# A planner that orders five engines is told other durations for its transfers

## The chip, the cores and the metric

The program runs on one core of one Trainium2 chip. The metric is the device time of one execution in microseconds (us). The matrix engine is called PE here, VectorE DVE, ScalarE ACT, GpSimd POOL, and SyncE, which issues all the transfers, SP.

## What is computed

```python
def _attn_ref(q, k, v):                      # (8, 12, 448, 64) float32 each
    scores = np.matmul(q, k.transpose(0, 1, 3, 2)) / np.sqrt(64) - np.log(448)
    return np.matmul(1.0 / (1.0 + np.exp(-scores)), v)
...
x = attn.transpose(0, 2, 1, 3).reshape(8, 448, 768)
h = x.transpose(0, 2, 1) @ U @ V             # U (448, 32), V (32, 448)
u = x + h.transpose(0, 2, 1)
y = u + np.maximum(u @ w_ch1, 0.0) @ w_ch2   # (768, 3072) and (3072, 768)
```

Sigmoid attention over 8 batches of 12 heads, a mixing of rank 32 along the sequence, and a feed-forward with a residual.

## The kernel before

**Stages.** The two feed-forward weights come as 48 pieces of 128x768 words (w_in), are decoded on DVE and ACT, split in two float16 halves and written to memory (scratch). Attention goes batch by batch in six pairs of heads. A pair of batches 0 to 2 is multiplied in float32; a pair of batches 3 to 7 (30 pairs) is first staged: four loads of keys and queries into a `qk` buffer (three of them) and loads of the values; on ACT a bound of each (L469, into `junk`); the bounds go out to memory (`far`, 128x3 words) and come back as one row on all partitions (`row`, 128x384, a single buffer); DVE reduces that row (L448), and after three small operations POOL and DVE write a high and a low float16 half of queries, keys and values into one of two `stg` buffers. PE then makes the scores, ACT the sigmoid (`at`, L675) and the high halves of the weights (`a`, L698 and L701), DVE the low halves (L416 out of L700 and L703), PE the values, ACT copies them to `u` (L707).

The feed-forward of batches 0 to 3 runs in groups of the weights, 18 matmuls for each block in (`ffn_in`, evacuated by ACT at L934 and L935 and by DVE at L936) and 12 for each block out (`ffn_out`, added to `ua` or `ub` by DVE at L955, which shows as L416). Batches 4 and 5, then 6 and 7, go through products of seven by a Strassen scheme (`product`), whose weight forms are made by `quarter_sums` and whose inputs lie in `ufar` (L1063) and are loaded into the freed `qk` and other buffers (L1089) when the last scores are done.

**What sets the order.** Nothing is written by hand in its final order. `Plan.op` notes each operation with its engine, a told cost, what it reads and writes, and a position; `Plan.order` then steps through a simulated time: the engine that can start first takes, of its operations that are ready, the one with the lowest position. A transfer takes its cost on SP, then its `dma` time on one common pipe (L208), and is there `LAND` later. The result is a fixed order on each of the five engines and a fixed choice of buffers. On the chip every engine works through its own list, waiting at semaphores.

```python
op("SP", 0.6 if n in (...) else 0.36, ..., land=land, dma=max(0.2, n / RATE))    # load(), L387
load(lambda: far.x, lambda: parts.x[:, :n], 0.08e6, kp, [far], pos)               # scale_by_dma, L445
load(lambda: row.x[...], lambda: far.x..., 0.2e6, [far], [row], pos)              # L446
```

With `RATE` 0.33e6 bytes per us and `LAND` 2.2 us. The positions come from some 45 numbers at the head of the file (L54 to L73).

## Time and profile before

| | |
|---|---|
| median of 3 runs | 1577.08 us (1575.58 to 1581.07) |
| the profiled execution | 1587.46 us |
| its span, first to last instruction | 1585.7 us |
| mean granted clock of PE | 0.996 |
| busy: PE, DVE, ACT, POOL | 98%, 70%, 49%, 23% |
| moved by DMA | 303.82 MB, 192 GB/s on average |

The page lists busy time by engine and by line. A busy PE is no proof that it is not held up elsewhere, so the rows below go from windows of the span to the waits of PE, and from these to the timeline, in which the bracket behind an instruction gives the idle time of its engine before it and what ended it. Lines such as L403, L413 and L416 are helpers; tiles tell what an instruction belongs to.

### The profile page before, as it was taken

How to read it: one execution, taken by the hardware profiler on the slowest of the kernel's cores; microseconds unless marked ns; L12 is line 12 of the kernel's file. 1: busy time of each engine (PE TensorE's matmuls, PEld its weight loads, DVE VectorE, ACT ScalarE, POOL GpSimd, SP SyncE). 2: the span in 40 equal slices, each digit the busy share in tenths (PEclk: the TensorE clock that was granted, in tenths of full speed). 3: DMA queues.
4: the chain of work that ended last, by engine and by line, in shares of the span. 5: the costliest groups of instructions: out<-in, count | busy, mean ns of one | idle time of the engine just before them, and what ended most of it. 6: DMA issues, size and time to landing. Idle time of an engine off the chain costs nothing.

```text
span 1585.7 us, 23387 instructions
## 1 busy us (share of the span) xinstructions
PE 1556.3 (98%) x8651; PEld 761.4 (48%) x8651; DVE 1110.7 (70%) x1831; ACT 774.2 (49%) x1269; POOL 358.6 (23%) x429
## 2 busy tenths in 40 slices
PE   8999999999999999899899999999999999999999
PEld 2334444454444454444444445555555555555554
DVE  3688888476676577687678776687767677565656
ACT  5566456445665547677676772342333614131210
POOL 0110000014541453122213325045552500000000
PEclk9999999999999999999999999999999999999999
DMA  9599777345667875667578447968683664323321
GB/s 268 162 291 335 238 240 263 126 121 149 201 158 202 218 273 148 174 157 190 142 216 223 140 142 261 302 221 256 205 265 121 243 233 142 114 105 130 115 105 70
DMA packets 217554, 303.82 MB, mean 192 GB/s; under 512 B 138336, under 2 KB 188384, under 8 KB 206176
## 3 DMA queue, kind: packets, MB, share of 16 engines
q1 hardware_dynamic: 217440, 302.33, 62.7%
q8 instruction: 68, 1.11, 0.3%
q14 instruction: 46, 0.38, 0.1%
HBM read 232.10 MB, written 76.04 MB: 194 GB/s over the span
## 4 chain that ended last, share of the span: by engine, by line
PE 77%; DMA 11%; DVE 5%; SPq 3%; issue 2%; ACT 2%; POOL 0%; ACTq 0%; POOLq 0%; DVEq 0%
PE banks L403 76%; DMA far<-tiny 3%; DMA w<-w_in 2%; DMA row__114<-far 2%; SPq L387 2%; DMA forms<-scratch 1%; DVE a L416 1%; SPq L989 1%; DMA w<-parked 1%; ACT at L675 1%; DMA qk__101<-q_in 1%; DMA w__92<-scratch 1%; DVE stg__109 L416 1%; PE banks L406 1%; DMA forms<-xnt 0%
## 5 line engine op out<-in xcount | busy, mean ns | idle before, releaser
L403 PEld LDWEIGHTS <-w__92 128*128 128x128 f16 x1683 | 163.5, 98 | 158.1 <-issue 8.1
L403 PEld LDWEIGHTS <-w__91 128*128 128x128 f16 x1620 | 157.4, 98 | 152.1 <-issue 7.9
L403 PEld LDWEIGHTS <-w__94 128*128 128x128 f16 x1620 | 156.5, 98 | 153.8 <-issue 11.3
L403 PEld LDWEIGHTS <-w__93 128*128 128x128 f16 x1557 | 151.6, 99 | 155.5 <-issue 21.7
L675 ACT ACTIVATE at<-banks,tiny 128x896 f32<-128x896 f32 x120 | 128.1, 1097 | 46.3 <-DVE a L416 20.0
L403 PE MATMUL banks<-h__96,w__94 128*128 128x448 f16 x696 | 141.7, 353 | 0.7 <-ACT h__95 L935 0.5
L416 DVE SCALAR_TENSOR_TENSOR a<-at,a 64x896 f16<-64x896 f32 (+1 forms) x120 | 134.9, 1135 | 10.3 <-ACT a L701 4.8
L403 PE MATMUL banks<-h__95,w__93 128*128 128x448 f16 x657 | 136.7, 361 | 4.6 <-DVE ua__73 L416 4.5
L413 POOL TENSOR_SCALAR tiny<-tiny 128x1 f32<-128x1 f32 (+1 forms) x90 | 33.4, 381 | 388.9 <-DVE tiny L413 359.0
L1010 POOL TENSOR_TENSOR w<-w 128x384 f32<-128x384 f32 x96 | 105.5, 1099 | 5.4
L403 PE MATMUL banks<-us__90,w__91 128*128 128x448 f16 x501 | 101.9, 353 | 0.4 <-DVE ub__82 L416 0.4
L403 PE MATMUL banks<-us__90,w__92 128*128 128x448 f16 x498 | 101.5, 353 | 0.0
L403 PE MATMUL banks<-us__89,w__92 128*128 128x448 f16 x474 | 95.5, 353 | 1.5 <-ACT r__97 L934 1.5
L403 PE MATMUL banks<-us__89,w__91 128*128 128x448 f16 x474 | 96.0, 353 | 0.0
L701 ACT ACTIVATE a<-at 128x896 f16<-128x896 f32 x90 | 82.7, 947 | 0.2
L448 DVE TENSOR_REDUCE tiny<-row__114 128x3 f32<-128x384 f32 x30 | 20.2, 674 | 71.8 <-DMA row__114<-far 71.8
L675 ACT ACTIVATE a<-banks,tiny 128x448 f32<-128x448 f32 (+1 forms) x72 | 62.6, 910 | 12.6 <-PE banks L403 12.4
L1006 POOL TENSOR_TENSOR w<-w 128x384 f32<-128x384 f16 x48 | 46.2, 992 | 95.5 <-DVE xnt L1014 61.7
L1013 ACT CAST xnt<-w 128x1536 f16<-128x1536 f32 x24 | 35.2, 1469 | 40.5 <-POOL w L1010 23.3
L934 ACT ACTIVATE r__97<-banks 128x448 f32<-128x448 f32 x48 | 25.8, 538 | 57.7 <-PE banks L403 56.2
L403 PEld LDWEIGHTS <-stg__108 64*128 64x128 f16 (+1 forms) x690 | 32.8, 102 | 42.8 <-issue 21.2
L403 PE MATMUL banks<-h__95,w__94 128*128 128x448 f16 x258 | 52.4, 353 | 0.0
(896 smaller groups left out, 2864.2 us busy)
## 6 DMA issues: line engine op xcount, KB each, us to landing
w<-w_in SPq DMA_DIRECT2D x48, 768.0 KB, 6.9
forms<-xnt SPq DMA_DIRECT2D x24, 768.0 KB, 4.8
w__92<-forms SPq DMA_DIRECT2D x13, 1344.0 KB, 5.7
w__91<-forms SPq DMA_DIRECT2D x12, 1344.0 KB, 6.4
w__94<-forms SPq DMA_DIRECT2D x12, 1344.0 KB, 6.4
w__93<-forms SPq DMA_DIRECT2D x11, 1344.0 KB, 5.8
forms<-scratch SPq DMA_DIRECT2D x144, 96.0 KB, 4.9
w__91<-scratch SPq DMA_DIRECT2D x7, 1536.0 KB, 8.3
```

The source lines that it names most:

```text
L387: op("SP", 0.6 if n in (D * S * 4, D * D * 4, D * P * 4) else 0.36, lambda: nc.sync.dma_start(out=dst(), in_=src()), reads, writes, pos, l ...
L403: plan.made.append(nc.tensor.matmul(*x, **y))
L406: plan.made.append(nc.tensor.transpose(**x))
L413: return eng.tensor_scalar(out=out, in0=in_, scalar1=s1, scalar2=s2, op0=op0, **kw)
L416: return nc.vector.scalar_tensor_tensor(out=out, in0=in0, scalar=s, in1=in1, op0=op0, op1=op1)
L448: dve(0.15 + n * 0.175, lambda: nc.vector.tensor_reduce(out=m(), in_=row.x[:, : n * P].rearrange("q (p n) -> q n p", n=n), axis=AX.X, op=A ...
L675: act(cost, lambda: nc.scalar.activation(out_(), in_(), AF.Sigmoid, bias=bias_s, scale=c if whole else c.x), kin + ["bias"] + kc, kout, pos)
L701: act(0.95, lambda a=a, to=to: nc.scalar.activation(half(a, 0), to.x, AF.Copy, scale=A_UP), kto, [(a, 0)], here + A_OFF)
L934: act(0.54, lambda: nc.scalar.activation(r.x, ph.x[:, :S], AF.Relu, scale=DOWN_H), [ph], [r], pos - EV_IN)
L1006: pool(1.0, lambda j=j: nc.gpsimd.tensor_tensor(out=t.x[:, j], in0=quarter(j, 0), in1=quarter(j, 1), op=ALU.add), [(w, j, 0), (w, j, 1)] i ...
L1010: pool(1.0, lambda o_=o_, x=x, y=y, sub=sub: nc.gpsimd.tensor_tensor(out=t.x[:, o_], in0=t.x[:, x], in1=t.x[:, y], op=ALU.subtract if sub ...
L1013: act(1.45, lambda: nc.scalar.copy(o.x[:, :, :, 0], t.x.rearrange(order)), [(t, j) for j in range(4)], [(o, 0)], pos)
```

## The change

The operations, their dependencies and their number stay as they are. What the planner is told changes:

- `load` looks the pipe time up in a table `PIPE` by the byte count and falls back to the rate. The far and row loads are now given as P * 6 and P * 1536 bytes (768 and 196,608) and so find entries of 2.2 and 1.3 us instead of 0.24 and 0.61. A key or query load is 0.53 instead of 0.35, the small loads of 64x64 and 64x128 words 0.13 and 0.1 instead of 0.2, the values of a staged pair 1.3 (they have the row's byte count) instead of 0.60. The byte counts of a weight piece (P * PIECE * 8, 2.5 us) and of a store of weight forms (P * 24 * P * 2, 1.92 us) are the same number, 786,432, so that the second entry holds for both.
- Told costs of small operations on POOL and DVE are changed, most of them lowered.
- An engine may take an operation that is ready up to `HOLD` later than the first; this is 0.029 us on PE and 0 elsewhere.
- The numbers that set the positions are all new, and six of them (`B0` to `B5`) shift the begin of each later batch.

```diff
+PIPE = {P * PIECE * 8: 2.5, D * S * 4: 0.53, D * D * 4: 0.13, D * P * 4: 0.1, P * 2 * WE * 2: 4.8, P * 42 * P * 2: 4.1, P * 24 * P * 2: 1.92, P * 6: 2.2, P * 1536: 1.3}
-SWITCH, TURN, LAND, RATE = 0.09, -1.137, 2.2, 0.33e6
+SWITCH, TURN, LAND, RATE = 0.09, -2.054, 2.2, 0.33e6
+HOLD_PE, HOLD_DVE, HOLD_ACT, HOLD_POOL, HOLD_SP = 0.029, 0.0, 0.0, 0.0, 0.0
-PREP, BOUNDS, VALUES, SECOND, MIXED = 20.269, 8.551, 2.056, 3.976, 7.545
+PREP, BOUNDS, VALUES, SECOND, MIXED = 19.043, 11.533, 1.917, 3.17, 7.744
...
-            i = min((x[1], x[2]) for x in now if x[0] <= t + 1e-9)[1]
+            _, i, t = min((x[1], x[2], x[0]) for x in now if x[0] <= t + HOLD(e) + 1e-9)
...
-        op("SP", ..., land=land, dma=max(0.2, n / RATE))
+        op("SP", ..., land=land, dma=PIPE.get(n, n / RATE))
...
-        load(lambda: far.x, lambda: parts.x[:, :n], 0.08e6, kp, [far], pos)
-        load(lambda: row.x[:, : n * P], ..., 0.2e6, [far], [row], pos)
+        load(lambda: far.x, lambda: parts.x[:, :n], P * 6, kp, [far], pos)
+        load(lambda: row.x[:, : n * P], ..., P * 1536, [far], [row], pos)
...
-        pool(0.35, lambda: ts(nc.gpsimd, inv.x, x(), ...), [e], [inv], pos)
+        pool(0.28, lambda: ts(nc.gpsimd, inv.x, x(), ...), [e], [inv], pos)
...
-                pool(1.5, lambda t=t, cut=cut: scaled(w.x[:, 0, cut], t.x, s.x), [t, s], [hi], at)
+                pool(1.0, lambda t=t, cut=cut: scaled(w.x[:, 0, cut], t.x, s.x), [t, s], [hi], at)
...
-                begun_ = [MIDDLE - SOONER + NP * d * (i - BEND * i * ...) for i in (j, j + 1)]
+                begun_ = [MIDDLE - SOONER + NP * d * (i - BEND * i * ...) + (B0, B1, B2, B3, B4, B5)[i] for i in (j, j + 1)]
```

The order moves at many places: of PE's 856 blocks of matmuls 420 stand elsewhere, nearly all by a few places. Three places follow; in the rows `tiny` are columns of one small tile, `stg__108` and `stg__109` the two staging buffers, `banks` the accumulators. The lines of the changed kernel are 4 higher.

DVE at 651 to 663 us (before), where one pair's low halves are staged and the next pair's row is due; before:

```order
L416 SCALAR_TENSOR_TENSOR ua__73<-banks_110,tiny,ua__73 128x448
L448 TENSOR_REDUCE tiny<-row__114 128x3
L416 SCALAR_TENSOR_TENSOR ua__74<-banks_111,tiny,ua__74 128x448
L416 SCALAR_TENSOR_TENSOR stg__108<-qk__102,tiny,stg__108 128x512
L416 SCALAR_TENSOR_TENSOR stg__108<-qk__102,tiny,stg__108 128x448
L416 SCALAR_TENSOR_TENSOR a<-at,a 128x896 x2
L416 SCALAR_TENSOR_TENSOR stg__108<-v__105,tiny,stg__108 128x512
L413 TENSOR_SCALAR tiny<-tiny 128x3
```

now:

```order
L420 SCALAR_TENSOR_TENSOR ua__73<-banks_111,tiny,ua__73 128x448
L420 SCALAR_TENSOR_TENSOR stg__108<-qk__102,tiny,stg__108 128x512
L420 SCALAR_TENSOR_TENSOR stg__108<-qk__102,tiny,stg__108 128x448
L420 SCALAR_TENSOR_TENSOR a<-at,a 128x896 x2
L420 SCALAR_TENSOR_TENSOR stg__108<-v__105,tiny,stg__108 128x512
L438 TENSOR_REDUCE tiny<-banks_111 128x1
L940 TENSOR_TENSOR h__96<-r__97,h__96 128x448
L452 TENSOR_REDUCE tiny<-row__114 128x3
```

The reduction of the next pair's row went from ahead of the two key and query halves to behind them, two splits of weights, the values, a small reduction and an evacuation of the feed-forward.

DVE at 750 to 759 us, where `ua__73` is the evacuation of a feed-forward block out; before:

```order
L416 SCALAR_TENSOR_TENSOR stg__108<-qk__102,tiny,stg__108 128x512
L416 SCALAR_TENSOR_TENSOR stg__108<-qk__102,tiny,stg__108 128x448
L416 SCALAR_TENSOR_TENSOR stg__108<-v__105,tiny,stg__108 128x512
L448 TENSOR_REDUCE tiny<-row__114 128x3
L434 TENSOR_REDUCE tiny<-banks_111 128x1
L413 TENSOR_SCALAR tiny<-tiny 128x3
L416 SCALAR_TENSOR_TENSOR a<-at,a 128x896
L413 TENSOR_SCALAR tiny<-tiny 128x1
L416 SCALAR_TENSOR_TENSOR ua__73<-banks_111,tiny,ua__73 128x448
```

now, around the same reduction:

```order
L417 TENSOR_SCALAR tiny<-tiny 128x1
L940 TENSOR_TENSOR h__96<-r__98,h__96 128x448
L442 RECIPROCAL tiny<-tiny 128x1
L832 TENSOR_TENSOR tiny<-tiny 128x1
L420 SCALAR_TENSOR_TENSOR ua__75<-banks_110,tiny,ua__75 128x448
L420 SCALAR_TENSOR_TENSOR ua__76<-banks_111,tiny,ua__76 128x448
L420 SCALAR_TENSOR_TENSOR w_107<-uc__87,tiny,w_107 128x448
L420 SCALAR_TENSOR_TENSOR a<-at,a 128x896 x2
L420 SCALAR_TENSOR_TENSOR w_107<-uc__86,tiny,w_107 128x448
L452 TENSOR_REDUCE tiny<-row__114 128x3
```

The staged halves stand nine rows and more above these, `ua__73` and `ua__74` of that group too; the reduction follows `ua__75` and `ua__76`.

ACT at 720 to 730 us, where `r__97` is the copy that frees a bank of the feed-forward; before:

```order
L675 ACTIVATE at<-banks_113,tiny 128x896
L675 ACTIVATE at<-banks_112,tiny 128x896
L698 ACTIVATE a<-at 128x896
L701 ACTIVATE a<-at 128x896
L469 ACTIVATE junk,tiny<-qk__103 128x448
L934 ACTIVATE r__97<-banks_110 128x448
L675 ACTIVATE at<-banks_113,tiny 128x896
L675 ACTIVATE at<-banks_112,tiny 128x896
```

now:

```order
L939 ACTIVATE h__96<-banks_110 128x448
L679 ACTIVATE at<-banks_113,tiny 128x896
L679 ACTIVATE at<-banks_112,tiny 128x896
L702 ACTIVATE a<-at 128x896
L705 ACTIVATE a<-at 128x896
L473 ACTIVATE junk,tiny<-v__105 128x512
L711 ACTIVATE uc__87<-banks_111,tiny 128x448
L679 ACTIVATE at<-banks_113,tiny 128x896
L679 ACTIVATE at<-banks_112,tiny 128x896
L705 ACTIVATE a<-at 128x896 x2
L852 ACTIVATE xnt<-banks_111 128x384
L473 ACTIVATE junk,tiny<-qk__103 128x448 x2
```

That `r__97` stands three rows above the first of these, and the bounds of `qk__103` come after both pairs of sigmoids.

## Rows read from the trace of the kernel before

**Rows 1.** The page: span, and busy time, share and count of PE
```profile
span 1585.7 us, 23387 instructions
...
PE 1556.3 (98%) x8651; PEld 761.4 (48%) x8651; DVE 1110.7 (70%) x1831; ACT 774.2 (49%) x1269; POOL 358.6 (23%) x429
```

**Rows 2.** Windows: stretch, length, busy us (count) of PE, PEld, DVE, ACT, POOL, clock, DMA, GB/s
```profile
0.00:125.00 125.00, 116.47 (x499) 42.41 (x499) 80.05 (x143) 75.25 (x121) 11.40 (x18) 1.00 0.80 246
125.00:480.00 355.00, 355.00 (x1944) 172.79 (x1943) 263.48 (x465) 195.21 (x330) 64.64 (x77) 1.00 0.67 203
480.00:870.00 390.00, 372.80 (x2346) 180.62 (x2345) 284.35 (x462) 257.45 (x414) 119.88 (x170) 0.98 0.72 193
870.00:1010.00 140.00, 140.00 (x844) 69.74 (x842) 97.58 (x145) 77.77 (x119) 45.04 (x50) 1.00 0.63 201
1010.00:1586.00 576.00, 572.02 (x3026) 295.83 (x3023) 385.23 (x619) 168.51 (x287) 117.59 (x115) 1.00 0.51 170
```

**Rows 3.** Waits of PE, 480 to 870 us: waiter, releaser, us in total, times, longest
```profile
PE banks L403 <- DVE ua__73 L416: 4.5, 1, 4.5
PE banks L403 <- DVE stg__108 L416: 4.4, 1, 4.4
PE banks L403 <- DVE xnt L416: 2.0, 2, 1.8
PE banks L406 <- DVE tiny L864: 1.8, 2, 1.6
PE banks L403 <- ACT r__97 L934: 1.5, 1, 1.5
```

**Rows 4.** Windows behind the two long stalls, the columns of rows 2
```profile
660.49:665.80 5.31, 5.31 (x19) 2.01 (x19) 3.92 (x11) 4.24 (x5) 2.30 (x6) 0.50 0.36 97
759.14:764.79 5.65, 5.65 (x16) 2.26 (x16) 3.94 (x9) 5.57 (x10) 1.92 (x3) 0.50 0.15 39
```

**Rows 5.** Timeline, 657 to 661 us: start, us, instruction [idle before <-what ended it]
```profile
657.94 0.66 DVE L448 TENSOR_REDUCE tiny<-row__114 128x3 f32<-128x384 f32 x1 [6.84 <-DMA row__114<-far]
...
660.49 2.05 PE L403 MATMUL banks<-stg__108 64*128 64x448 f16 x10 [4.44 <-DVE stg__108 L416]
```

**Rows 6.** Timeline, 756 to 760 us
```profile
756.51 0.66 DVE L448 TENSOR_REDUCE tiny<-row__114 128x3 f32<-128x384 f32 x1 [4.40 <-DMA row__114<-far]
...
759.14 3.14 PE L403 MATMUL banks<-h__95,w__93 128*128 128x448 f16 x8 [4.54 <-DVE ua__73 L416]
```

**Rows 7.** Timeline, 502 to 511 and 728 to 730 us
```profile
502.29 0.63 ACT L469 ACTIVATE junk<-v__104 128x512 bf16<-128x512 f32 x1 [4.11 <-DMA v__104<-v_in]
...
504.05 0.74 PE L403 MATMUL banks<-stg__109 64*128 64x448 f16 x6 [0.63 <-ACT at L675]
...
510.91 0.32 PE L406 MATMUL banks<-ident,tiny 128*128 128x128 f32 x1 [1.61 <-DVE tiny L864]
...
728.16 0.58 ACT L469 ACTIVATE junk<-qk__103 128x448 bf16<-128x448 f32 x1 [3.97 <-DMA qk__103<-k_in]
...
729.31 1.86 PE L403 MATMUL banks<-us__89,w__92 128*128 128x448 f16 x9 [1.45 <-ACT r__97 L934]
```

**Rows 8.** DVE's wait for rows; row loads (KB, median); landing, far and row together
```profile
DVE tiny L448 <- DMA row__114<-far: 71.8, 22, 6.8
...
row__114<-far SPq DMA_DIRECT2D x30, 192.0 KB, 4.4
...
DMA to landing us min/median/max: 2.1/4.3/10.0
```

**Rows 9.** Timeline, 996 to 1000 us, and loads into qk__102 (KB, median landing)
```profile
996.49 6.99 PE L403 MATMUL banks<-h__96,w__93 128*128 128x448 f16 x36
...
999.48 0.91 SPq L1089 DMA_DIRECT2D qk__102<-ufar  x2
...
qk__102<-ufar SPq DMA_DIRECT2D x2, 224.0 KB, 4.5
```

**Rows 10.** Window 100 to 150 us, the columns of rows 2
```profile
100.00:150.00 50.00, 49.85 (x247) 21.77 (x245) 40.81 (x77) 33.07 (x56) 0.00 (x0) 1.00 1.05 346
```

More of the change, by code (lines that the diff above doesn't have):

```diff
@@ L57 @@
 TOGETHER = (2, 3, 4, 5)
-BEND = 0.363
+BEND = 0.397
 DIRECT = ()
@@ L61 @@
 MM = 0.1895
-SWITCH, TURN, LAND, RATE = 0.09, -1.137, 2.2, 0.33e6
+PIPE = {P * PIECE * 8: 2.5, D * S * 4: 0.53, D * D * 4: 0.13, D * P * 4: 0.1, P * 2 * WE * 2: 4.8, P * 42 * P * 2: 4.1, P * 24 * P * 2: 1.92, P * 6: 2.2, P * 1536: 1.3}
+SWITCH, TURN, LAND, RATE = 0.09, -2.054, 2.2, 0.33e6
 TINY = 235
-ROOM0, ROOM, AHEAD, BEFORE, D1, SOONER = 79.692, 36.616, 50.594, 84.968, 3.22, 70.551
-PREP, BOUNDS, VALUES, SECOND, MIXED = 20.269, 8.551, 2.056, 3.976, 7.545
-LOW_POOL = ()
-MIXED1, MIX_1 = 4.346, 0.294
-MIX_2, EV_IN, EV_OUT, A_OFF = 11.221, 32.25, 5.736, 0.065
-START, DECODE = 33.635, 57.84
-U_AT, U_STEP = 3.311, 4.227
-LEAD, SUMS, STEP_K, STEP_I, FFN_LEAD = 5.231, 24.217, 6.947, 6.876, 4.0
+B0, B1, B2, B3, B4, B5 = 2.934, -0.318, -0.301, -2.832, -1.273, 1.274
+HOLD_PE, HOLD_DVE, HOLD_ACT, HOLD_POOL, HOLD_SP = 0.029, 0.0, 0.0, 0.0, 0.0
+HOLD = lambda e: {"PE": HOLD_PE, "DVE": HOLD_DVE, "ACT": HOLD_ACT, "POOL": HOLD_POOL, "SP": HOLD_SP}[e]
+ROOM0, ROOM, AHEAD, BEFORE, D1, SOONER = 89.279, 30.792, 47.233, 54.769, 4.497, 70.468
+PREP, BOUNDS, VALUES, SECOND, MIXED = 19.043, 11.533, 1.917, 3.17, 7.744
+LOW_POOL = ()
+MIXED1, MIX_1 = 1.829, -0.567
+MIX_2, EV_IN, EV_OUT, A_OFF = 11.002, 33.543, 3.656, 0.056
+START, DECODE = 30.42, 56.642
+U_AT, U_STEP = 3.172, 3.581
+LEAD, SUMS, STEP_K, STEP_I, FFN_LEAD = 5.196, 28.387, 3.783, 5.28, 4.0
 ORDER = "iiiioiooiioiooiioiooiooo"
@@ L386, in load @@
     def load(dst, src, n, reads, writes, pos, land=LAND):
-        op("SP", 0.6 if n in (D * S * 4, D * D * 4, D * P * 4) else 0.36, lambda: nc.sync.dma_start(out=dst(), in_=src()), reads, writes, pos, land=land, dma=max(0.2, n / RATE))
+        op("SP", 0.6 if n in (D * S * 4, D * D * 4, D * P * 4) else 0.36, lambda: nc.sync.dma_start(out=dst(), in_=src()), reads, writes, pos, land=land, dma=PIPE.get(n, n / RATE))
     def dve(cost, fn, reads, writes, pos):
@@ L444, in scale_by_dma @@
         row, far = plan.tile("row", ROW), plan.tile(f"far{n}", FAR[n])
-        load(lambda: far.x, lambda: parts.x[:, :n], 0.08e6, kp, [far], pos)
-        load(lambda: row.x[:, : n * P], lambda: far.x.rearrange("p n -> (p n)").partition_broadcast(P), 0.2e6, [far], [row], pos)
+        load(lambda: far.x, lambda: parts.x[:, :n], P * 6, kp, [far], pos)
+        load(lambda: row.x[:, : n * P], lambda: far.x.rearrange("p n -> (p n)").partition_broadcast(P), P * 1536, [far], [row], pos)
         m, x = (lambda: e.x[:, :n]), (lambda: e.x[:, n : 2 * n])
@@ L701, in pair @@
                 act(0.95, lambda a=a, to=to: nc.scalar.activation(half(a, 0), to.x, AF.Copy, scale=A_UP), kto, [(a, 0)], here + A_OFF)
-                dve2(1.16, lambda a=a, to=to: rest(half(a, 1), to.x, A_UP, half(a, 0)), kto + [(a, 0)], [(a, 1)], here + A_OFF)
+                dve2(1.11, lambda a=a, to=to: rest(half(a, 1), to.x, A_UP, half(a, 0)), kto + [(a, 0)], [(a, 1)], here + A_OFF)
             keys += [(a, 0), (a, 1)]
@@ L837, in mix_half @@
         op("SP", 3.7, lambda: nc.sync.dma_start_transpose(out=xt.x, in_=xs.x.rearrange("p c x s -> p (c x s)")),
-           [(xs, i, x) for i in range(3) for x in range(2)], [xt], pos + 1.0, land=LAND, dma=0.9)
+           [(xs, i, x) for i in range(3) for x in range(2)], [xt], pos + 1.0, land=LAND, dma=0.2)
         tp, tt = plan.tile("av", PS_[b], False), plan.tile("th", TH)
@@ L989, in quarter_sums @@
                 op("SP", 0.6, lambda n_=n_, r=r, c=c, x=x: nc.sync.dma_start(out=far(n_, x), in_=cut(far_w, r, c, x)),
-                   [("scratch", i, g)], [("forms", i, n, n_, x)], pos, land=LAND, after=copy_after, dma=0.49)
+                   [("scratch", i, g)], [("forms", i, n, n_, x)], pos, land=LAND, after=copy_after, dma=0.4)
                 done.append(("forms", i, n, n_, x))
@@ L1013, in quarter_sums @@
         act(1.45, lambda: nc.scalar.copy(o.x[:, :, :, 0], t.x.rearrange(order)), [(t, j) for j in range(4)], [(o, 0)], pos)
-        dve2(1.9, lambda: nc.vector.tensor_tensor(out=o.x[:, :, :, 1], in0=t.x.rearrange(order), in1=o.x[:, :, :, 0], op=ALU.subtract),
+        dve2(1.77, lambda: nc.vector.tensor_tensor(out=o.x[:, :, :, 1], in0=t.x.rearrange(order), in1=o.x[:, :, :, 0], op=ALU.subtract),
              [(t, j) for j in range(4)] + [(o, 0)], [(o, 1)], pos)
@@ L1283, in fused_kernel @@
             kg_of(b, g, at + 10.0)
-        if g in FORMS.get(b, ()) and n >= first_pass:
+        if g in FORMS.get(b, ()) and (n >= first_pass or (b, g) == (1, NG - 1)):
             for i in range(2):
```

10 lines of the change are left out of this document (5 added, 5 removed).

## The prediction

> **What bounds the kernel now.** I read the page first, then windows by stage, then PE's waits by stage, then the timeline around the longest of them. TensorE (PE) is busy for 1556.3 of 1585.7 us [rows 1], so only what it waits can be won; the set of matmuls is the same after the change. The windows show where it waits [rows 2]: in the first 125 us it is busy 116.47 (idle 8.53), from 125 to 480 and from 870 to 1010 not one idle us, from 1010 on only the 4 us in which the last stores drain, and in the 390 us between 480 and 870 it is busy 372.80. So 17.20 us of idle time lie in one stretch: the attention of batches 3 to 7, beside the feed-forward of batches 1 to 3.
>
> PE's waits there are of ten kinds, the five largest 14.2 us [rows 3]. The timeline tells what is behind them, and it is one pattern: an engine that works strictly in its written order stands at an instruction whose transfer has not landed, and what PE needs is queued behind it. At 650 to 660 us VectorE (DVE) stands 6.84 us at the reduction of the broadcast row (L448) of one pair; behind it stands the low half of the staged keys (stg__108) of the pair before, for which PE then waits 4.44 us [rows 5]. At 754 DVE stands 4.40 us at L448, and the evacuation of ua__73, which frees a bank, is late: 4.54 us of PE [rows 6]. At 510 L448 holds up L864 behind it, 1.61 us of PE; at 502 and at 728 ScalarE (ACT) stands 4.11 and 3.97 us at a bound (L469) that needs a load, with the sigmoid and the copy r__97 behind it: 0.63 and 1.45 us of PE [rows 7]. DVE waits for the row 71.8 us in all, at 22 of its 30 reductions [rows 8]; most of that never reaches PE.
>
> The two long stalls cost twice: right after each, PE runs at a granted clock of 0.50 (1.2 instead of 2.4 GHz) for 5.31 and 5.65 us of full work [rows 4]. Half of that, 5.5 us, is lost. The stretch thus loses 17.2 + 5.5 = 22.7 us in the profiled execution.
>
> **How that stands to the runs.** The profiled execution took 1587.46 us, 1.76 more than its span; the median of the runs is 1577.08, 10.4 less. No row shows the shorter runs. The rest of the span is either without waits or (start, last stores) ordered the same, so I put the difference into this stretch: a plain run loses some 22.7 - 10.4 = 12.3 us there, 0.54 of the profile's loss.
>
> **What the change removes.** The planner sets the written order from told durations. For the small hop to memory (far) it was told 0.36 of issue, 0.08e6/0.33e6 = 0.24 of pipe and 2.2 to land, 2.80 us; for the broadcast row 0.36 + 0.61 + 2.2 = 3.17; 5.97 for the two, one after the other. The trace has 4.3 as the median of the two kinds together, so some 8.6 for both, and up to 10.0 for one [rows 8]. Now it is told 4.76 and 3.86, together 8.62. So the reduction stood some 2.6 us too early for a typical pair and now shouldn't; a slow transfer can still be late. The order shows it at the places that cost most:
> - at 655 the reduction stood right ahead of both halves of the staged keys; now these, two splits of the attention weights and the values stand ahead of it. The 4.4 go, and 2.7 of half clock with them.
> - at 754 it moves behind sixteen other instructions, and the ua__73 evacuation goes far ahead of it. The 4.5 go, and 2.8 of half clock.
> - at 510 L864 now stands ahead of the reduction: 1.6.
> - at 728 the bound moves behind r__97 (1.5), and at 502 behind the sigmoids (0.6).
> Sum: 4.4 + 4.5 + 1.6 + 1.5 + 0.6 = 12.6 of idle time and 5.5 of clock, 18.1 of the 22.7. I let the other 4.6 stand, the 2.0 at xnt among them: the store ahead of that one is told 0.46 us less than before (below), which rather speaks for more.
>
> **What it adds.** The planner fills the time anew, so other instructions become the late ones. One is seen in the order: where the products of batches 4 and 5 begin. Before, the score matmuls that free the qk buffers end at 996.49, the third load into these buffers is issued at 999.48 and such loads take 4.5 us, so the first product could start 7.5 us after the scores; 36 feed-forward matmuls (6.99 us) and a values block lay between, and nothing waited [rows 9]. Now 24 such matmuls (4.66 us) and seven of 384 columns (some 1.2 by the same rate) lie between: 5.8 us, short by 1.7. The bounds are 0 (loads that land quicker) and 1.7 plus 2.8 of half clock; I take 1.7. Of other new late places the trace of before cannot tell. Lower bound 0; the nearest rows for the upper one are the waits of 1.5 to 2.0 us there [rows 3], six of them, some 10. I take 2.8, two waits of about 1.4: by rows 8 some transfers will land later than even the new figures say, but the typical one no longer does. New in all: 4.5.
>
> Nothing else weighs. The first 60 us have the same order on PE and SyncE, so the 4.3 of start and the other early waits stay. The durations of small operations that change (a POOL scaling of 1.0 us where 1.5 was told, and the like) only sharpen the order. The tail after 1010 has no waits to win.
>
> **The sum.** Against the profiled execution: 1587.46 - 18.1 + 4.5 = 1573.9. For the runs, each term in the share 0.54: 1577.08 - 9.8 + 2.4 = 1569.7; the 1.7 at the products comes from an order in which every run would wait, so I count it fully, + 0.8: **1570.5 us**. Floor: with no loss left in the stretch and none new, 1587.46 - 22.7 = 1564.8.
>
> **A rule against it.** The far and row transfers land after 2.1 us at the quickest, 4.3 in the middle, 10.0 at the slowest [rows 8], so most of them take longer than their own move needs. The Trainium skill (DMA: Bandwidth & Descriptors, "Anatomy of one DMA — SWDGE (gpsimd) path") says of DMAs issued by GpSimd that about 2.0 us are fixed, for setup and completion, and only the bytes scale; by it, taken over to this queue, far is 2.0 and the row 2.0 + 196608/436e3 = 2.45, 4.45 together, so what the planner was told before was already enough, and 2.2 us of pipe for a 1.5 KB transfer books time in which the pipe is free. The trace agrees at its minimum and not at its median. What this mechanism gives here is the first rival.
>
> **Rivals.** First, the new figures are no better where it counts: far's 2.2 us is latency, not occupancy, so everything planned behind it is believed late, and a transfer stuck behind a 1.5 MB fetch (10.0 us) is missed as before. Then new waits of the size of the old take their place, 9.8 of gain against as much loss: 1577, between 1573 and 1581. For it: 22 waits on the row show a wide spread, which one figure can't hold. Against it: in five of five places looked at the order moves the right way.
>
> Second, slower: the reduction is now put so late that the pair's own scores wait. After it come three small operations, two POOL scalings and two on DVE before the keys are staged, 4.5 us by the costs in the code; where less PE work than that lies between the reduction's new place and the pair's scores, PE waits, and the same delay meets the next pair, since the row has one buffer. At 2 us for seven of the 30 pairs and once long enough for the half clock it costs 14 + 2.7 = 16.7, from which the 9.8 come off: 1577 + 6.9 = 1584. It decides from the point where such waits cost more than 9.8. Against it: where seven instructions now go ahead of it, at 655, the reduction stood 6.84 us for its row anyway [rows 5].
>
> Third, early weights: two entries of the new table have the same byte count (786,432), and the later, 1.92 us, holds for the 48 weight pieces too, told 2.38 before. The trace moves 346 GB/s at its fullest, 2.27 us a piece [rows 10]. Eight pieces by 0.35 is 2.8 us on the first groups, where PE now has next to no idle time: 1573.3, inside the range.
>
> Fourth, more: all of the loss goes and nothing new comes: 1565.
>
> **How the numbers follow.** Forecast (with the third rival in it) 0.58, its own range 1565.5 to 1574.5; waits that change places 0.27; slower 0.09; the floor case 0.06. 0.3% of 1577.08, about what a measurement can tell, is 4.7 us: below 1572.4 is faster. Of the forecast 0.54 lies below that and 0.04 above; the floor gives 0.06, the first rival 0.02: faster 0.62. Same: 0.04 + 0.25 = 0.29. Slower: 0.09. The range leaves out half of the floor case at the bottom and the slower rival on top: 1564 to 1580.
>
> **What would show it.** In the profile after: DVE's wait for the row well under 71.8 us; no PE wait over 4 us and no slice of granted clock under 1.0 between 480 and 870; PE idle there at 5 to 9 instead of 17.2; a wait of 1 to 2 us at the first product, near 980. Wrong: PE waits of 1 to 5 us at scores whose stg is late (second rival), or the same DVE and ACT standing at L448 and L469, now lines 452 and 473, in other places (first rival); idle PE between 60 and 125 (third).

## The result

The changed kernel takes 1564.66 us (median of 4 runs, 1560.01 to 1566.72) where the kernel before took 1578.16 beside it (4 runs): ratio 0.9906, 95% interval 0.9887 to 0.9925. Five more runs, made beside the experiments below, have a median of 1562.23 against 1582.72 (9 runs): ratio 0.9881, interval 0.9858 to 0.9904. So it is faster by 13.5 us in the first comparison and 20.5 in the second; the forecast was 6.6.

The page of the changed kernel, its span and its busy times, which answer to [rows 1]. TensorE (PE) does the same 8651 matmuls in 7.5 us less busy time:

```profile
span 1558.2 us, 23417 instructions
...
PE 1548.8 (99%) x8651; PEld 759.9 (49%) x8651; DVE 1112.4 (71%) x1831; ACT 776.1 (50%) x1269; POOL 351.5 (23%) x429
```

The windows, with the stretches and columns of [rows 2] (the last one is longer than the span; what matters in it is the busy time):

```profile
0.00:125.00 125.00, 119.79 (x517) 44.27 (x518) 81.92 (x149) 79.81 (x126) 11.39 (x18) 1.00 0.84 260
125.00:480.00 355.00, 354.64 (x1940) 172.61 (x1940) 264.68 (x463) 192.10 (x327) 59.77 (x77) 1.00 0.65 198
480.00:870.00 390.00, 389.77 (x2497) 190.81 (x2494) 298.41 (x489) 278.02 (x455) 118.94 (x172) 1.00 0.74 205
870.00:1010.00 140.00, 140.00 (x828) 70.75 (x826) 99.46 (x154) 67.89 (x98) 42.56 (x48) 1.00 0.70 219
1010.00:1590.00 580.00, 544.58 (x2879) 281.43 (x2877) 367.89 (x580) 158.23 (x268) 118.81 (x114) 1.00 0.46 156
```

Between 480 and 870 us PE's idle time went from 17.20 us to 0.23, and the clock there is 1.00 throughout. These are all waits of PE in the changed kernel (waiter, releaser, us in total, times, longest); of the ones in [rows 3] none is left:

```profile
PE banks L407 <- DMA qk__101<-q_in: 4.3, 1, 4.3
PE banks L407 <- ACT a L679: 1.0, 2, 0.6
PE banks L407 <- ACT h__96 L939: 0.4, 1, 0.4
PE banks L407 <- ACT at L679: 0.2, 1, 0.2
```

VectorE's (DVE) wait for the rows and the time from issue to landing of far and row together, which answer to [rows 8]:

```profile
DVE tiny L452 <- DMA row__114<-far: 16.3, 13, 3.7
...
DMA to landing us min/median/max: 2.1/4.0/11.2
```

The wait fell from 71.8 us to 16.3, while the transfers land hardly more quickly than before (2.1/4.3/10.0). It is the order that changed, not the transfers. At the two places of [rows 5, 6] the timeline of DVE (start, us, instruction, idle before it and what ended it) now reads:

```profile
642.45 2.14 DVE L420 SCALAR_TENSOR_TENSOR stg__108<-qk__102,tiny,stg__108 128x512 f16<-128x512 f32 x2 [0.19 <-POOL stg__108 L417]
...
650.92 0.70 DVE L452 TENSOR_REDUCE tiny<-row__114 128x3 f32<-128x384 f32 x1 [2.93 <-DMA row__114<-far]
...
744.77 0.67 DVE L452 TENSOR_REDUCE tiny<-row__114 128x3 f32<-128x384 f32 x1
```

At 650.92 DVE still stands 2.93 us for a row, but the staged keys, which stood behind the reduction before, were finished well ahead of it: PE has no wait there. At 744.77 the row is there when DVE comes.

**Where the 27.5 us between the two profiled spans are** (1585.7 to 1558.2): 17.0 of idle time between 480 and 870; 7.5 of busy time, of which 5.5 are the half clock of [rows 4] and 2.0 I can't place; 3.3 of idle time in the first 125 us (8.53 to 5.21); less 0.4 that is new between 125 and 480. The first experiment shows that the 3.3 belong to the execution and not to the change.

### The profile page after: what moved, and what is told of

Same layout as the page of the kernel before. It is cut to its first block, busy times and chain, and to the rows that moved or that the text cites. A ratio compares the mean times of both kernels' runs of the same rounds, so it can differ in the third digit from the quotient of the medians.

```text
span 1558.2 us, 23417 instructions
## 1 busy us (share of the span) xinstructions
PE 1548.8 (99%) x8651; PEld 759.9 (49%) x8651; DVE 1112.4 (71%) x1831; ACT 776.1 (50%) x1269; POOL 351.5 (23%) x429
## 4 chain that ended last, share of the span: by engine, by line
PE 57%; ACT 0%; DMA 0%; issue 0%; DVE 0%; SPq 0%; ACTq 0%
PE banks L407 57%; DMA v__105<-v_in 0%; ACT at L679 0%; PE banks L410 0%; ACT w L839 0%; ACT a L705 0%; DVE ub__79 L420 0%; SPq L391 0%; ACT junk L473 0%; ACTq L473 0%; DVE tiny L832 0%; ACT uc__83 L711 0%; DVE tiny L442 0%
## 5 line engine op out<-in xcount | busy, mean ns | idle before, releaser
L679 ACT ACTIVATE at<-banks,tiny 128x896 f32<-128x896 f32 x120 | 127.0, 1098 | 42.0 <-DVE a L420 18.9
L407 PE MATMUL banks<-h__96,w__94 128*128 128x448 f16 x690 | 139.7, 353 | 0.0
L407 PE MATMUL banks<-h__95,w__93 128*128 128x448 f16 x678 | 136.9, 353 | 0.4 <-ACT h__96 L939 0.4
L417 POOL TENSOR_SCALAR tiny<-tiny 128x1 f32<-128x1 f32 (+1 forms) x90 | 30.0, 342 | 354.4 <-DVE tiny L417 328.3
L407 PE MATMUL banks<-us__89,w__92 128*128 128x448 f16 x498 | 101.3, 353 | 0.0
L407 PE MATMUL banks<-us__89,w__91 128*128 128x448 f16 x501 | 101.2, 353 | 0.0
L407 PE MATMUL banks<-us__90,w__91 128*128 128x448 f16 x471 | 95.1, 353 | 0.0
L407 PE MATMUL banks<-us__90,w__92 128*128 128x448 f16 x471 | 94.6, 353 | 0.0
L679 ACT ACTIVATE a<-banks,tiny 128x448 f32<-128x448 f32 (+1 forms) x72 | 63.0, 910 | 27.6 <-PE banks L407 27.5
L938 ACT ACTIVATE r__98<-banks 128x448 f32<-128x448 f32 x48 | 26.0, 541 | 70.6 <-PE banks L407 68.1
L938 ACT ACTIVATE r__97<-banks 128x448 f32<-128x448 f32 x48 | 25.9, 539 | 60.9 <-PE banks L407 60.7
L407 PE MATMUL banks<-h__95,w__94 128*128 128x448 f16 x264 | 54.3, 353 | 0.0
L407 PE MATMUL banks<-h__96,w__93 128*128 128x448 f16 x249 | 51.3, 353 | 0.0
```

The lines of the kernel that those rows point to most:

```text
L407: plan.made.append(nc.tensor.matmul(*x, **y))
L417: return eng.tensor_scalar(out=out, in0=in_, scalar1=s1, scalar2=s2, op0=op0, **kw)
L679: act(cost, lambda: nc.scalar.activation(out_(), in_(), AF.Sigmoid, bias=bias_s, scale=c if whole else c.x), kin + ["bias"] + kc, kout, pos)
L938: act(0.54, lambda: nc.scalar.activation(r.x, ph.x[:, :S], AF.Relu, scale=DOWN_H), [ph], [r], pos - EV_IN)
```

## The experiments

Twelve experiments ran on three chips, two of them the two kernels once more, and beside each there are runs of the kernel before on the same chip (medians 1581.42 of 27, 1582.72 of 9, 1582.21 of 17), so that the ratios are what to compare. **Theory:** what the scheduler is told of the far and row loads decides; it sets the reduction so far behind its loads that nothing PE needs stands behind a waiting DVE. **Rivals:** the gain lies in the position numbers; or in the other told durations; or the profiled execution of before was a chance one.

### The kernel before, once more

Edit: none.

> The kernel before once more, nothing changed: a second profiled execution, to see which idle stretches of TensorE belong to the kernel and which to one execution. If the waits at the row loads belong to the order of the work, VectorE stands at L448 behind row loads for 50 to 75 us in all again, and TensorE idles 8 to 18 us between 480 and 870 us, at the same places (near 655 and 754) though not always for as long. If the profiled execution of before was a chance one, the idle there falls under 6 us with nothing changed. The start (0 to 125 us) tells the same of the 3.3 us that the changed kernel won there: if they belong to the order, about 8.5 us of idle stand there again; if to the execution, 5 to 6.

It took 1580.75 us (span 1579.0). Its windows (columns as in [rows 2]) and the two largest waits of PE in the middle:

```profile
0.00:125.00 125.00, 119.58 (x513) 43.78 (x514) 80.96 (x147) 77.95 (x124) 11.42 (x18) 1.00 0.82 252
...
480.00:870.00 390.00, 374.11 (x2373) 182.27 (x2372) 282.02 (x459) 261.06 (x423) 122.39 (x172) 0.99 0.73 193
```
```profile
PE banks L403 <- DVE ua__73 L416: 5.2, 1, 5.2
...
PE banks L403 <- DVE stg__108 L416: 3.4, 1, 3.4
```

Between 480 and 870 PE idles 15.89 us, 8.6 of them at the same two places, and DVE stands 62.4 us at L448 in all. So the waits belong to the order of the work. The start differs: 5.42 us of idle instead of 8.53, with not one instruction changed. Of the eight profiles of kernels that keep the first 125 us as the kernel before or the changed one has them, five idle 5.2 to 6.0 us there and three 8.2 to 9.6, and both orders have both. So the start belongs to the execution, and makes some 3 us of its time.

### The reductions 2.65 us later, all else as before

The scheduler of the kernel before runs with its own numbers and yields its order. Then each chain of L448 to L452 (the reduction, the mask, POOL's scaling and the reciprocal) is put where the scheduler had work that starts 2.65 us later; whatever depends on it, or takes over its buffer, follows as far as it must.

```
+            by = 2.65
+            for i in range(first, last):
+                at = self.planned[i] + by
+                n = next((n for n, t in enumerate(times) if t >= at), len(done))
+                key[i] = (n - 0.5, key[i][1])
...
+        return sorted(done, key=lambda i: key[i])
...
-        for i in self.order():
+        for i in self.moved(self.order()):
```

> The kernel before in its own order and with its own numbers; only the 30 chains of L448 to L452 (the reduction over a row and its three small followers) stand 2.65 us later in the order of the work, what depends on them follows only as far as it must. If the gain comes from where VectorE meets the row loads, its wait there falls from 71.8 us to under 30, TensorE idles under 7 us between 480 and 870 us with no stretch at half clock, and the runs come to 1564 to 1571 us (ratio about 0.993). If the late chains make the stg tiles late in turn, VectorE's wait falls as much, but TensorE and ScalarE stand at stg__108 and stg__109, and the runs come to 1576 to 1586. If the gain lies in the positions of everything else, the wait falls and the runs stay within 1574 to 1579.

1571.55 us (10 runs), ratio 0.9946 (0.9927 to 0.9966): a little under half of the whole gain. From its groups of instructions (busy, mean ns, then the idle time before them) and its windows:

```profile
L475 DVE TENSOR_REDUCE tiny<-row__114 128x3 f32<-128x384 f32 x30 | 20.4, 678 | 18.9 <-DMA row__114<-far 18.9
```
```profile
480.00:870.00 390.00, 379.15 (x2413) 185.13 (x2411) 289.08 (x467) 264.90 (x428) 130.70 (x179) 1.00 0.71 193
```

DVE's wait fell nearly as far as in the changed kernel (18.9 against 16.3), the two long stalls are gone, but 10.85 us of PE's idle time stayed in the middle (15.89 to 17.20 before; under 7 was expected), now in many short waits: 2.4 for the w tiles, 1.9 at r__97, 1.6 at xnt, 1.6 at a scale, 1.2 at ub__78. The profiled execution, 1575.92, is the second slowest of the ten, so the median run may well idle less. Placing the reductions alone is not the whole of it. That the rest was planned for the old places is my reading; no run tests it by itself.

### Only the tight reductions later

As above, but only chains that stand less than 8.62 us behind the issue of their far load are moved, each to that distance.

```
-            by = 2.65
+            by = max(0.0, self.planned[self.far_of[first]] + 8.62 - self.planned[first])
```

> As the one above, but only the chains that stand less than 8.62 us behind the issue of their far load (the least distance that the changed kernel leaves) are moved, each to that distance; the others stay. If the tight ones alone made the waits, VectorE's wait at the rows is under 35 us and the runs come to 1563 to 1570 us, at or below the uniform shift. If the later chains cost the stg tiles their time, this one costs less than the uniform shift, 1574 to 1580. If the gain lies elsewhere, 1574 to 1579.

1578.8 us (12 runs), ratio 0.9988 (0.9971 to 1.0005): no gain that can be told from nothing, though DVE's wait fell to 46.1 us. The timelines of DVE and PE near 750 us show why. Here, with the tight ones moved:

```profile
749.10 0.66 DVE L476 TENSOR_REDUCE tiny<-row__114 128x3 f32<-128x384 f32 x1 [4.52 <-DMA row__114<-far]
...
751.00 0.68 DVE L442 SCALAR_TENSOR_TENSOR ua__73<-banks,tiny,ua__73 128x448 f32<-128x448 f32 x1
```
```profile
751.73 7.39 PE L429 MATMUL banks<-h__95,w__93 128*128 128x448 f16 x24 [5.14 <-DVE ua__73 L442]
```

And in the kernel with all of them 2.65 us later:

```profile
747.11 0.67 DVE L442 SCALAR_TENSOR_TENSOR ua__73<-banks,tiny,ua__73 128x448 f32<-128x448 f32 x1
749.22 0.67 DVE L475 TENSOR_REDUCE tiny<-row__114 128x3 f32<-128x384 f32 x1 [1.43 <-DMA row__114<-far]
```
```profile
747.84 2.43 PE L429 MATMUL banks<-h__95,w__93 128*128 128x448 f16 x12 [0.80 <-DVE ua__73 L442]
```

The wait at the reduction isn't itself the cost. The evacuation of ua__73, which frees a bank for PE, stood behind it in the one order and ahead of it in the other: 5.14 us of PE's time against 0.80.

### The changed kernel with the reductions 2.65 us earlier

The same edit on the changed kernel, `by = -2.65`.

> The changed kernel in its own order; only the 30 chains of L452 to L456 stand 2.65 us earlier in the order of the work (about the distance from their loads that the kernel before had), everything else as it is. If the gain comes from where VectorE meets the row loads, its wait there goes from 16.3 us back to 55 to 80, TensorE's idle between 480 and 870 us from 0.2 to 5 to 17 us, and the runs from 1565 to 1570 to 1578. If the gain lies in the positions of everything else, VectorE waits as long but TensorE doesn't, and the runs stay within 1562 to 1567.

1576.64 us (12 runs), ratio 0.9965 (0.9948 to 0.9983), where the changed kernel has 0.9881: some 70% of the gain is gone. DVE waits 65.5 us at the rows again, and PE's idle time in the middle is back at 8.06 us:

```profile
480.00:870.00 390.00, 381.94 (x2452) 186.48 (x2450) 290.81 (x477) 273.26 (x441) 127.43 (x168) 1.00 0.72 199
```

In this profile as much waiting of DVE as before costs PE half of what it cost before. But the profiled execution, 1571.15 us at a granted clock of 1.00, is the second quickest of the twelve; the median is 5.5 us longer, and eleven of the twelve were granted 0.996 to 0.999. So the half is a low figure, and by the medians some 14 of the 20 us are back. That fewer urgent instructions stand behind the reductions in this order would fit, but wasn't shown.

### The changed kernel, once more

Edit: none.

> The changed kernel once more, nothing altered, with more executions and a second profile, as the measure for the others. Two executions of the kernel before, one row of waits apart, have shown 8.5 and 5.4 us of idle TensorE before 125 us, so what the changed kernel won there belongs to the execution: 5 to 8 us are expected. If its gain between 480 and 870 us belongs to the order, TensorE idles under 3 us there again and VectorE waits 12 to 25 us at the row loads; the runs should come to 1564 to 1570. If the first profile was a lucky one, 4 to 8 us of idle and 25 to 45 us at the row loads.

1562.23 us (5 runs), ratio 0.9881. DVE waits 19.7 us at the rows; the start has 5.39 us of idle; in the middle there is none at all:

```profile
480.00:870.00 390.00, 390.00 (x2501) 190.90 (x2499) 298.08 (x490) 278.49 (x453) 118.07 (x172) 1.00 0.74 206
```

Set against the second profile of the kernel before, which has the same start (5.42), this is the change alone: spans 1579.0 and 1560.0, 19.0 us apart, of which 15.9 are idle time in the middle, 4.2 are busy time (3.3 of it two stretches at half clock, shown under the hardware below), and 1.1 is new idle time between 125 and 480.

### The weight pieces told 2.5 us

```
-PIPE = {P * PIECE * 8: 2.5, ...
+PIPE = {P * PIECE * 8 + 1: 2.5, ...
...
-            load(..., P * PIECE * 8, [], [w64],
+            load(..., P * PIECE * 8 + 1, [], [w64],
```

> The changed kernel, but the scheduler is told 2.5 us of pipe for the w_in pieces of 786,432 bytes, as its table first says, instead of the 1.92 that a later entry of the same size puts in its place. If the gain came in part from the start, where these pieces are loaded, the idle before 125 us rises by 1 to 3 us and the runs by as much, to 1567 to 1571. If the start is left alone by it and all lies in the middle, the order after 480 us is nearly the same and the runs stay within 2 us of the changed kernel.

1560.76 us (5 runs), ratio 0.9866 (0.9846 to 0.9887), which can't be told from the changed kernel's 0.9881. The start idles 5.09 us, the middle 0.00. The prediction's third rival falls: the two entries of one size in the table cost nothing and won nothing.

### The new position numbers on the old durations

Of the changed kernel, every told duration as before:

```
-... dma=PIPE.get(n, n / RATE))
+... dma=max(0.2, n / RATE))
...
-        load(lambda: far.x, lambda: parts.x[:, :n], P * 6, kp, [far], pos)
+        load(lambda: far.x, lambda: parts.x[:, :n], 0.08e6, kp, [far], pos)
...
-        pool(0.28, ...
+        pool(0.35, ...
```

> The changed kernel's position numbers, with every duration that the scheduler is told as in the kernel before (the table of pipe times, the small operations and the offset of the choice on TensorE taken back). If the told durations carry the gain, the reductions stand close behind their loads again: VectorE waits 55 to 90 us at L448, TensorE idles 8 to 20 us between 480 and 870 us, and the runs come to 1573 to 1582. If the position numbers carry it, VectorE's wait is under 35 us and the runs come to 1564 to 1570. If the numbers only fit the durations that they came with, it is slower than both, over 1585, with waits that neither kernel has.

1625.84 us (4 runs), ratio 1.0276 (1.0250 to 1.0301). The expectation names the offset of the choice on PE among what is taken back; that is wrong: the offset (TURN) and the margin stayed as in the changed kernel and count with the position numbers here. DVE waits 56.7 us at the rows, and PE stands in the middle (21.42 us) and, for the first time, behind it (10.11, and some 12 more behind 1010), at a clock of 0.95 to 0.98 in the two stretches:

```profile
480.00:870.00 390.00, 368.58 (x2282) 179.06 (x2280) 265.41 (x424) 245.55 (x390) 126.98 (x169) 0.98 0.69 184
870.00:1010.00 140.00, 129.89 (x738) 63.59 (x735) 90.36 (x145) 69.80 (x120) 31.73 (x44) 0.95 0.66 204
```

The position numbers do not carry the gain; of the three outcomes expected it is the last, numbers that fit only the durations that they came with.

### The new durations on the old position numbers

Of the kernel before, every told duration as in the changed one (the reverse of the edit above; offset and margin as before).

> The kernel before's position numbers, with every duration that the scheduler is told as in the changed kernel. If the told durations carry the gain, VectorE's wait at the row loads falls under 30 us and the runs come to 1565 to 1572. If the position numbers carry it, the wait stays over 50 us and the runs within 1576 to 1584. If the numbers only fit the durations that they came with, the wait at the rows falls as told, yet the kernel is slower than both, over 1585, with waits at other places.

1596.39 us (4 runs), ratio 1.0085 (1.0063 to 1.0108): slower than both kernels, and yet

```profile
480.00:870.00 390.00, 386.83 (x2459) 189.21 (x2458) 290.68 (x479) 267.35 (x436) 110.67 (x169) 1.00 0.70 198
870.00:1010.00 140.00, 123.48 (x704) 60.06 (x702) 81.96 (x119) 64.64 (x93) 46.44 (x50) 0.94 0.59 187
```

The middle has lost its idle time (3.17 us left), with the position numbers of before and DVE waiting only 10.5 us at the rows. What it won there it loses behind 870 us, where the kernel before had not one idle us [rows 2]: 16.52 us, the longest 4.3 at the weights of a group (w__92) and 3.4 at scores whose bank a sigmoid had yet to free.

### Far and row alone

The kernel before, with two told figures changed and nothing else (their sizes are only the keys):

```
+PIPE = {P * 6: 2.2, P * 1537: 1.3}
...
-... dma=max(0.2, n / RATE))
+... dma=PIPE.get(n, max(0.2, n / RATE)))
```

> The kernel before with only the far and row loads told as in the changed kernel (2.2 and 1.3 us of pipe); all other told durations, and the position numbers, as before, and the whole order computed anew. If these two figures are what took the idle out of 480 to 870 us, VectorE's wait at the rows falls under 20 us and TensorE idles under 5 us in that stretch, as it did with all the new figures on the old numbers (10.5 and 3.2 us), whatever waits then come up behind 870 us. If the other figures have a share, 6 to 12 us of idle stay in that stretch (10.9 stayed when the chains alone were moved). In either case the runs come out at or over the kernel before, ratio 1.000 to 1.015, since the numbers that set the first products are not refitted.

1599.55 us (4 runs), ratio 1.0102 (1.0078 to 1.0126). The windows:

```profile
480.00:870.00 390.00, 390.00 (x2470) 191.31 (x2470) 282.64 (x452) 261.44 (x420) 124.22 (x171) 1.00 0.70 197
870.00:1010.00 140.00, 120.32 (x697) 58.53 (x696) 94.10 (x149) 77.84 (x118) 36.22 (x48) 0.93 0.66 191
```

In the middle PE has not one idle us left, on two figures alone. Unlike the shift by hand, the scheduler places all else anew around the later reductions. Behind 870, 19.68 us of new idle time undo it, and some 7 more behind 1010. The attention itself runs later here: the last row load is issued at 989 us, in the kernel before at 914, in the changed one at 884. And 8.1 of the 19.68 us are scores whose staged tiles are late, the longest of them behind a row that DVE stands for:

```profile
992.49 0.69 DVE L449 TENSOR_REDUCE tiny<-row__114 128x3 f32<-128x384 f32 x1 [3.01 <-DMA row__114<-far]
```
```profile
997.69 0.56 PE L404 MATMUL banks<-stg__108 64*128 64x448 f16 x2 [4.35 <-POOL stg__108 L414]
```

So with the old position numbers the two figures move the waits rather than remove them.

### The changed kernel without those two figures

```
-        load(lambda: far.x, lambda: parts.x[:, :n], P * 6, kp, [far], pos)
-        load(lambda: row.x[:, : n * P], ..., P * 1536, [far], [row], pos)
+        load(lambda: far.x, lambda: parts.x[:, :n], 0.08e6, kp, [far], pos)
+        load(lambda: row.x[:, : n * P], ..., 0.2e6, [far], [row], pos)
```

> The changed kernel with the far and row loads told as before (by their bytes and the one rate), all else as changed, and the whole order computed anew. If these two figures made the gain, VectorE waits 50 to 75 us at the rows again, TensorE idles 6 to 17 us between 480 and 870 us, and the runs come to 1572 to 1585. If the other figures and the position numbers hold the gain, the wait at the rows rises and TensorE idles under 3 us there; 1562 to 1568.

1604.16 us (4 runs), ratio 1.0123 (1.0096 to 1.0150), more than either theory said. DVE waits 58.1 us at the rows, and nearly all of the loss is in the middle, with little behind it:

```profile
480.00:870.00 390.00, 365.04 (x2304) 176.41 (x2303) 279.80 (x451) 262.05 (x421) 117.26 (x161) 0.97 0.71 189
870.00:1010.00 140.00, 139.81 (x833) 70.03 (x831) 91.25 (x145) 75.56 (x113) 46.43 (x58) 1.00 0.60 182
```

The profiled execution, 1597.29, is the quickest of the four. The old pattern is back: an evacuation behind a reduction that stands for its row, and PE behind the evacuation.

```profile
548.69 0.66 DVE L452 TENSOR_REDUCE tiny<-row__114 128x3 f32<-128x384 f32 x1 [6.20 <-DMA row__114<-far]
...
549.46 0.68 DVE L420 SCALAR_TENSOR_TENSOR ub__79<-banks,tiny,ub__79 128x448 f32<-128x448 f32 x1
```
```profile
550.19 3.41 PE L407 MATMUL banks<-h__96,w__94 128*128 128x448 f16 x12 [3.88 <-DVE ub__79 L420]
```

A wait of 4.3 us at xnt (504 us) has the same form; the cause of the longest, 7.5 us for w at 702 us, is not shown.

### The margin of the choice on TensorE

```
-HOLD_PE, HOLD_DVE, HOLD_ACT, HOLD_POOL, HOLD_SP = 0.029, 0.0, 0.0, 0.0, 0.0
+HOLD_PE, HOLD_DVE, HOLD_ACT, HOLD_POOL, HOLD_SP = 0.0, 0.0, 0.0, 0.0, 0.0
```

> The changed kernel with the margin of the choice on TensorE set from 0.029 us to nothing: of the instructions that could start, only those that could start first are compared by position. If the margin is a small thing of its own, VectorE's wait at the rows stays under 25 us, the idle between 480 and 870 us under 4, and the runs within 1560 to 1567. If the position numbers fit the margin as they fit the durations, new waits of TensorE of 5 to 25 us come up, most of them outside 480 to 870, and the runs come to 1568 to 1590.

1588.32 us (10 runs), ratio 1.0031 (1.0013 to 1.0049): 0.029 us in a rule of choice make the whole gain come or go. The middle is as good as in the changed kernel (0.38 us idle, 17.7 at the rows); the loss is elsewhere: 5.8 us of idle time between 125 and 480, 9.2 in the start, half clock behind some of the stalls, and the largest two waits, both behind 870 us (at 977 and 1260):

```profile
PE banks L407 <- DMA w__92<-forms: 5.7, 1, 5.7
PE banks L407 <- DMA w<-w: 5.6, 1, 5.6
```

### Later still

The changed kernel with its 30 chains 1.3 us later, `by = 1.3`.

> The changed kernel in its own order; only the 30 chains of L452 to L456 stand 1.3 us later still. If the distance from the loads is now as large as it should be, VectorE's wait at the rows falls from 16 to 20 us to about 8 but TensorE has nothing left to win there (0.2 us of idle between 480 and 870), while the stg tiles come later, and the runs stay within 1560 to 1568, not under the changed kernel. If there is still a gain in distance, the runs fall by 2 us or more. If the later chains make the stg tiles late, waits of TensorE of 3 to 8 us at stg__108, stg__109 or the tiny scales come up and the runs come to 1566 to 1574.

1566.42 us (6 runs), ratio 0.9884 (0.9862 to 0.9907), the changed kernel's own. DVE still waits 15.9 us (8 were expected), at ten rows instead of thirteen, and the middle idles 0.75. More distance brings nothing and costs nothing. With PE at 99% there is little left: 1549.7 of the 1560.0 us of the changed kernel's second profile are matmuls, 4.2 the first load, 3.7 the last stores.

## Where the prediction failed: the mechanism held, the size did not

The direction, the mechanism and the five places were right, but the gain is two to three times the 6.6 us that were forecast. The step that failed is the share 0.54, by which a plain run was to lose only 12.3 of the 22.7 us: the second profiled execution, some 2 us quicker than the median of all later runs, loses 19.2 there. Two more terms were mis-sized: of the 4.6 us that were to stay 0.2 stayed, and of the 4.5 that were to be new 0.6 to 1.3 came. That the time still lies in the range is luck rather than the sum's merit: it lies under the forecast's own 1565.5 to 1574.5, at the end that was left open for the fourth rival, and the five later runs, 1562.23, lie below the whole range. By its own steps:

- **The loss of 22.7 us in one stretch** [rows 2, 4] held. A second execution has 15.9 of idle and 3.3 of clock there, 19.2.
- **What is removed, 18.1, with 4.6 let stand.** The five places went as said, each with its cause: the staged keys and the evacuation of ua__73 now stand ahead of the reduction, and 12.6 of idle time and 5.5 of clock are gone. The 4.6 that were to stay went as well (0.2 left, 0.0 in the second profile). I had read them as waits of their own; the far and row run shows that they go with the same two figures, which alone empty the stretch to 0.00, while shifting the same reductions by hand leaves 10.85. In all six profiles of orders that the scheduler laid with the new far and row figures the stretch idles 0.0 to 3.2 us, in all four with the old ones 15.9 to 25.0. The likely reason is that the scheduler doesn't only move the late instruction but fills the whole stretch anew; that is my reading, and no run tests it by itself.
- **What is new, 4.5.** Measured 0.2 at most between 480 and 1010 and 0.4 to 1.3 between 125 and 480. The 1.7 at the first product did not come. I had let the third load into the qk buffers be issued 3.0 us behind the last scores, as in [rows 9]. In the changed kernel the scores (first row below) end where the next row begins, at 967.35, and the third load is issued 0.26 us behind that; the products that read the two buffers (the last two rows of PE) start without a wait:

```profile
966.11 1.31 PE L407 MATMUL banks<-stg__108 64*128 64x448 f16 x12
967.35 4.71 PE L407 MATMUL banks<-h__96,w__93 128*128 128x448 f16 x24
...
973.04 1.30 PE L407 MATMUL banks<-qk__101,w__92 128*128 128x448 f16 x6
974.18 0.73 PE L407 MATMUL banks<-qk__102,w__92 128*128 128x448 f16 x3
```
```profile
966.64 0.92 SPq L1093 DMA_DIRECT2D qk__101<-ufar  x2
967.61 0.91 SPq L1093 DMA_DIRECT2D qk__102<-ufar  x2
```

The work between scores and product was counted rightly; that the gap between scores and loads would keep its length was not. That waits can spring up behind 870 us was a sound worry all the same: the new durations, all of them or the two alone, bring 16.5 to 19.7 us of them there with the old position numbers, and the margin of 0.029 us decides over two of 5.6 and 5.7. The position numbers of the changed kernel avoid them; the trace of before does not tell that.
- **The early waits stay.** True of the kernel, not of its profiles: the start idles 8.53 and 5.42 us with the same code.
- **The share 0.54** was the step that cost most. I took the profiled execution of before to be 10.4 us over a plain run and charged all of that to the stretch, so that each term counted half. Two things were wrong. The three runs shown were low ones: 53 later runs on three chips have medians of 1581.4 to 1582.7 and reach from 1573.7 to 1590.3, so that the profile is 5 to 6 us over the middle, not 10.4. The runs also list a mean granted clock: its median over the 53 is 0.997, the profile's 0.996, so by these two figures a plain run has most of the half clock too. And of the 6.7 us between the two profiles of before, 3.1 lie in the start and 3.5 in the stretch. With 19.2 of loss in such an execution, all of it removed and 1.1 new, the terms give 18.1; the spans of the second pair of profiles are 19.0 apart.

**The rivals.** The first (a transfer's latency told as pipe time only moves the waits) is what the far and row run shows: the middle won wholly, and more lost behind it. It falls for the change as a whole, whose own position numbers leave 0.6 to 1.3 us of idle time between 125 and 1010. The prediction set beside it a rule of the Trainium skill (DMA: Bandwidth & Descriptors, "Anatomy of one DMA — SWDGE (gpsimd) path"), by which about 2.0 us of a transfer that GpSimd issues are fixed and the two hops, taken over to this queue, would take an estimated 4.45 us together. In the trace of before the quickest far hop, 2.1 us, agrees, but the row hop alone lands after 3.1 us at the quickest and a median of 4.4, and from the issue of the far load to the landing of the row it is 6.5 us at the least and 8.7 in the median. So none of the 30 pairs kept the 5.97 us that the planner had been told, the new 8.62 is close to the median, and the measurement decides. The second (reductions too late) falls for the changed kernel with the run that set them 1.3 us later still, at no cost; its sign, scores whose staged tiles are late, shows in the far and row run (8.1 us). The third (pieces told too short) falls with the run that told them 2.5 us. The fourth, all of the loss gone and nothing new, was given 0.06 at 1565 and is nearly what happened.

**Open.** Which of the other told durations (key and query loads, stores and transposes, the small operations) and which of the position numbers keep the stretch behind 870 us free wasn't separated; the runs show only that neither set does it without the other. The 2.0 us less of busy time beside the half clock (0.9 in the second pair of profiles) are not explained.

## What to carry to other kernels

On an engine that works in its written order, count not how long it stands at a late transfer but what stands behind it: 65 us of such waits cost PE 8 us in one order (in a quick execution), 62 to 72 cost it 16 to 17 in another, and one instruction ahead of or behind a reduction made 0.80 or 5.14 us. When a scheduler lays the order, tell it the latency that the trace shows under load, and fit its other numbers again afterwards: the right figures on numbers fitted to wrong ones were slower than the wrong figures. Before a profile's loss is scaled to the runs, take a second profile: three runs were too few to say where the middle lies.

## What the hardware showed

The clock after a stall was the least expected. PE's granted clock fell to 0.50 (1.2 instead of 2.4 GHz) behind the long stalls, but for how long, and behind how short a stall, varied. First the second profile of before, behind stalls of 3.43 and 5.23 us (columns as in [rows 4]):

```profile
656.15:659.70 3.55, 3.55 (x15) 1.38 (x15) 3.52 (x8) 2.48 (x3) 0.68 (x2) 0.53 0.30 76
755.48:759.30 3.82, 3.82 (x12) 1.57 (x12) 2.97 (x7) 3.79 (x8) 0.75 (x2) 0.57 0.15 36
```

These are 3.5 to 3.8 us of slow work where the first profile had 5.3 and 5.7 behind 4.4 and 4.5 us. Then, from the run with all reductions 2.65 us later, a stall of 2.17 us and what follows it:

```profile
766.79 0.78 PE L429 MATMUL banks<-w,ua 128*128 128x384 f16 x3 [2.17 <-DMA w<-w]
```
```profile
766.79:770.70 3.91, 3.91 (x13) 1.82 (x14) 1.01 (x2) 1.82 (x3) 1.31 (x3) 0.56 0.51 145
```

And from the changed kernel with its reductions earlier, one of 2.42 us with no fall at all:

```profile
659.26 0.95 PE L433 MATMUL banks<-a,stg__109 128*64 128x448 f16 x8 [2.42 <-DVE tiny L464]
```
```profile
659.26:664.00 4.74, 4.74 (x41) 2.61 (x41) 4.64 (x11) 1.62 (x4) 4.02 (x6) 1.00 0.54 155
```

Nor is a longer stall sure to be followed by a slower stretch. In the run without the margin:

```profile
176.42 0.36 PE L407 MATMUL banks<-vst,xnt 128*128 128x448 f16 x1 [3.41 <-DVE xnt L420]
```
```profile
176.42:182.42 6.00, 6.00 (x34) 3.40 (x35) 5.99 (x15) 2.68 (x4) 0.00 (x0) 1.00 0.48 107
```

So in these rows a stall of 2.2 to 2.4 us added 1.7 us of lost work, or nothing; those of 3.4 to 5.2 us in the middle of the kernel before added 1.6 to 2.8, and one of 3.41 elsewhere nothing. None of the stalls under 2 us in the two kernels was followed by a slower stretch.

The spread of the far and row transfers is not all chance. In the trace of before 12 of the 60 were issued while a 1.5 MB fetch of a group's weights was still in flight; they landed after a median of 8.3 us, the other 48 after 4.1. In the changed kernel it is 20 after 7.7 and 40 after 3.7. One told figure can't hold both kinds, and in the changed kernel DVE still waits 16.3 us for rows.
